# Block 0 of a fused attention and gated feed-forward kernel: another way of masking, another order of weight loads, and its projection moved

## The chip, the cores and the metric

The kernel runs on one core of one Trainium2 chip. The metric is device time in microseconds (us), from the first to the last work of the core as the device reports it; lower is better. Before the change it is 230.33 us, the median of 8 runs that lie between 230.22 and 230.37.

A core has a matrix engine (PE), a vector engine (DVE), a scalar engine (ACT), a general engine that here mostly issues transfers (POOL) and a synchronisation engine that also issues transfers (SP). Each takes its instructions in the order in which the program gives them to it.

## The reference: what is computed

Two stages. The first is causal linear attention with a decay per head, over 4 batches, 8 heads, 768 positions and 64 features per head. In blocks:

```python
intra = (q_b @ k_b.T) * Dmask          # Dmask[i,j] = lam**(i-j) where i >= j, else 0
out_b = intra @ v_b + (q_b * lam**(i+1)) @ state
state = lam**block * state + (k_b * lam**(block-1-j)).T @ v_b
```

The result, as x with 3072 rows of 512, goes through a gated feed-forward layer:

```python
out = (sigmoid(x @ w_gate) * (x @ w_val)) @ w_out     # 512 -> 1536 -> 512
```

## The kernel before, in words

The sequence is cut into 6 blocks (n = 0 to 5) of 128 positions. A block holds all 4 batches, so its feed-forward part has 512 rows. All matrix work is in bf16 with fp32 sums; the inputs are fp32 in memory and are mostly cast by the transfer that loads them.

**Attention of a block**, per batch: q and k are transposed (`t_`, line 202; from block 2 on by transposing transfers, `xbar`, line 229), copied to SBUF (`e_q`, `e_k`), multiplied to scores (`piece_s`, line 238), masked by DVE (`piece_m`, line 249, two operations of 128x512 per batch), and multiplied with v (`piece_a`, line 266). `piece_i` (line 255) adds the part that comes from the state, `piece_x` copies the sum to the feed-forward's input XT, and `piece_c` makes the state's update from `KD`, which is k times a decay, made on ACT by `piece_kd` (line 116). The decay is split over two factors: q is multiplied by lam^(i+1) (`lamq`) in `e_q`, and the mask holds lam^-(j+1) under the diagonal. From block 1 on, batches 2 and 3 have their even and odd heads swapped between the partition halves, and use `lamqs` and `decs`, copies of `lamq` and `dec` with the halves exchanged by four small transfers.

**Feed-forward of a block**: 12 groups `piece_gv` (line 308), each of 4 gate and 4 value matmuls of 128x128 by 512, a sigmoid on ACT and a product on DVE that gives HT; then 4 output tiles `piece_po` (line 324), each of 12 matmuls over all 12 HT, a copy on ACT and a transfer out. In `piece_po` the twelfth matmul of a tile needs the last HT.

**Order.** The order on every engine is written out by hand: first block 0's attention, interleaved with matmuls on zeros (`zeros`) that keep PE busy, then a list `plan` of units. A unit is a `gv` group or an output tile, with smaller pieces behind it. An instruction that waits holds back everything behind it on its engine. Block 0's groups carry block 1's attention (`behind`, lines 451 to 459); groups 0 to 3 of block 1 come next, then block 0's four output tiles, then groups 4 to 11 of block 1 (lines 478 to 490). From block 2 on the order is: 12 groups, the next block's attention, 4 output tiles.

**Loads.** POOL issues q, k, v and all weights in a written order (lines 143 to 163 and 385 to 395), and the transfers land in that order. Before a POOL transfer is issued, the eighth one before it must have landed. After block 1's v come the output weights WO in two row halves of 0.75 MB (as bf16), then k and q of block 2. `next_loads(2)` (line 403) puts block 2's two transposing transfers on SP and, after a gate on POOL, the loads of v of block 2 and of k, q of block 3. SP also issues every output transfer.

Of the kernel before, what the change touches and what calls it, by code (L numbers as in the profile page):

```python
# [16 lines left out]
def kernel(  # L17
# [23 lines left out]

    const = ctx.enter_context(tc.tile_pool(name="const", bufs=1))
    qkv = ctx.enter_context(tc.tile_pool(name="qkv", bufs=5))
    hwp = ctx.enter_context(tc.tile_pool(name="hwp", bufs=4))
    qtp = ctx.enter_context(tc.tile_pool(name="qtp", bufs=3))
    kdp = ctx.enter_context(tc.tile_pool(name="kdp", bufs=2))
    trsb = ctx.enter_context(tc.tile_pool(name="trsb", bufs=3))
# [23 lines left out]
    def swapped(n, b):  # L71
        return n > 0 and b >= NB2
# [7 lines left out]
    def rows_of(u):  # L80
        return slice(u * 64, (u + 1) * 64)
# [22 lines left out]
        nc.gpsimd.dma_start(out=WG[:, :, fs], in_=wg_r[:, :, fs])  # L104
        nc.gpsimd.dma_start(out=WV[:, :, fs], in_=wv_r[:, :, fs])

    def load_wo(f0, f1):
        fs = slice(f0, f1)
        nc.gpsimd.dma_start(out=WO[:, fs, :], in_=wo_r[:, fs, :])

    KD = {}

# [13 lines left out]
    jn = const.tile([128, 2], FP32, tag="jn")  # L126
    ip1 = const.tile([128, C], FP32, tag="ip1")
    tri = const.tile([128, C], FP32, tag="tri")
    Sb = stp.tile([128, HP, B, 64], BF16, tag="Sb", name="Sb")
    lam_bc = const.tile([128, H], FP32, tag="lam_bc")  # L130

# [2 lines left out]
    def load_hw(c, b, eng):  # L134
# [9 lines left out]
    nc.scalar.preload_act_table_set("natural_log_exp_and_others")  # L144
    nc.vector.memset(ident, 0.0)
    nc.vector.memset(Sb, 0.0)  # L146
    nc.vector.memset(tri, 0.0)
    make_identity(nc, ident, nomemset=True)
    nc.gpsimd.iota(ip1, pattern=[[1, C]], base=1, channel_multiplier=0,
                   allow_small_or_imprecise_dtypes=True)  # L150
    load(0, "k", 2, 4)
# [10 lines left out]
    load_gv(2, 4)  # L162
    load_gv(4, 6)

    lnp = const.tile([128, HP], FP32, tag="lnp")
    for u in range(2):
        us = slice(u * 64, (u + 1) * 64)
        nc.scalar.activation(lnp[us, :], lam_bc[us, u::2], AF.Ln)
    lamq = const.tile([128, HP, C], BF16, tag="lamq")
    for hp in range(HP):  # L170
        nc.scalar.activation(lamq[:, hp, :], ip1, AF.Exp, scale=lnp[:, hp:hp + 1])
    lamqs = const.tile([128, HP, C], BF16, tag="lamqs")
    lnl = const.tile([128, H], FP32, tag="lnl")
    nc.scalar.activation(lnl, lam_bc, AF.Ln)
    pk = const.tile([128, H], FP32, tag="pk")
    nc.scalar.activation(pk, lnl, AF.Exp, scale=jn[:, 0:1])
    kds = const.tile([128, H], FP32, tag="kds")
    dec = const.tile([128, HP], FP32, tag="dec")
    decs = const.tile([128, HP], FP32, tag="decs")
    mask = const.tile([128, 2, HP, C], FP32, tag="mask")  # L180

    def tables_late():
        nc.scalar.activation(kds, lnl, AF.Exp, scale=jn[:, 1:2])
        nc.scalar.activation(dec, lnp, AF.Exp, scale=float(C))
        nc.scalar.preload_act_table_set("sigmoid_and_others")
        for o, i in ((lamqs, lamq), (decs, dec)):
            for u in range(2):
                nc.sync.dma_start(out=o[rows_of(u)], in_=i[rows_of(1 - u)])

    def make_mask():  # L190
        nc.vector.tensor_tensor(
            out=mask, in0=tri.unsqueeze(1).unsqueeze(1).to_broadcast([128, 2, HP, C]),
            in1=pk.rearrange("p (hp u) -> p u hp", u=2).unsqueeze(3).to_broadcast([128, 2, HP, C]),
            op=ALU.mult)

# [4 lines left out]
    def t_(c, n, bs):  # L202
        ps = ps_at.tile([128, len(bs), HP, C], BF16, name="t" + c, tag="ps")
        for i, b in enumerate(bs):
            for hp in range(HP):
                nc.tensor.transpose(ps[:, i, hp, :], T_[c, n][:, b, 2 * hp:2 * hp + 2, :], ident)  # L206
        (tqs if c == "q" else tks)[n, bs[0]] = ps

    def e_q(n, bs):
        w = len(bs)  # L210
        src = tqs[n, bs[0]] if n < FIRST_XBAR else QT[n][:, bs[0]:bs[0] + w]
        t = trsb.tile([128, 2, HP, C], BF16, tag="QS", name="QS")
        nc.vector.tensor_tensor(out=t[:, :w], in0=src,  # L213
                                in1=(lamqs if swapped(n, bs[0]) else lamq).unsqueeze(1).to_broadcast([128, w, HP, C]), op=ALU.mult)
        for i in range(w):
            QS[n, bs[i]] = t[:, i]

# [8 lines left out]
    def cast_hw(c, b):  # L226
        nc.vector.tensor_copy(T_[c, 0][:, b], H32[c, b])
# [21 lines left out]
    def piece_m(n, b):  # L249
        MT[n, b] = mtp.tile([128, 2, HP, C], BF16, tag="MT", name="MT")  # L250
        for u in range(2):
            nc.vector.tensor_tensor(out=MT[n, b][:, u], in0=SP[n, b][u],  # L252
                                    in1=mask[:, 1 - u if swapped(n, b) else u], op=ALU.mult)

    def piece_i(n):
        for b in range(B):
# [64 lines left out]
        HT[n, ft] = htp.tile([128, TCH], BF16, tag="ht", name="ht", bufs=2 * NFT)  # L321
        nc.vector.tensor_mul(HT[n, ft], sg, vp)  # L322

    def piece_po(n, tt, cuts=(0, 512)):
        ob = osb.tile([128, DM], FP32, tag="ob", name="ob")
        rows = out[tt * S + n * C:tt * S + (n + 1) * C, :]
        for j, (c0, c1) in enumerate(zip(cuts, cuts[1:])):
            po = ps_ff.tile([128, DM], FP32, name="po", tag="ff")
            for ft in range(NFT):
                nc.tensor.matmul(po[:, :c1 - c0], lhsT=HT[n, ft][:, tt * 128:(tt + 1) * 128],  # L330
                                 rhs=WO[:, ft, c0:c1], start=(ft == 0), stop=(ft == NFT - 1))
            if j:
                nc.vector.tensor_copy(ob[:, c0:c1], po[:, :c1 - c0])
            else:
                nc.scalar.copy(ob[:, c0:c1], po[:, :c1 - c0])  # L335
            nc.sync.dma_start(out=rows[:, c0:c1], in_=ob[:, c0:c1])

# [4 lines left out]
            nc.tensor.matmul(zps, lhsT=Sb[:, 0, 0:2, :], rhs=Sb[:, 0:2], start=True, stop=True)  # L344

    zeros(9)
    for b in range(2):
        cast_hw("k", b)
        t_("k", 0, [b])
        e_k(0, [b])  # L350
        zeros(3 if b == 0 else 0)
    make_mask()
    for b in range(2):
        t_("q", 0, [b])
        e_q(0, [b])
    zeros(1)
    for b in range(2):
        piece_s(0, [b])
        piece_m(0, b)
    t_("k", 0, [2, 3])  # L360
    e_k(0, [2, 3], parts=2)
    zeros(2)
    t_("q", 0, [2, 3])
    e_q(0, [2, 3])
    tables_late()
    zeros(3)
    for b in range(2, 4):
        piece_s(0, [b])
        piece_m(0, b)
    for b in range(2):  # L370
        piece_a(0, [b])
        piece_x(0, [b], nc.scalar)
# [3 lines left out]
    zeros(1)  # L376
    piece_a(0, [3])
    piece_x(0, [3], nc.vector)
    zeros(2)

    for n in range(2):
        make_kd(n)
    load_gv(6, 8)
    load(1, "k", 0, 2)
    load(1, "q", 0, 2)
    load_gv(8, 10)
    load(1, "k", 2, 4)
    load(1, "q", 2, 4)  # L390
    load_gv(10, 12)
    load(1, "v")
    load_wo(0, 6)
    load_wo(6, 12)
    load(2, "kq")

    gates = const.tile([128, 2], BF16, tag="gates")
# [19 lines left out]
    def gv(n, ft, *more):  # L417
        unit(lambda: piece_gv(n, ft), *more)

    def po(n, tt, *more, cuts=(0, 512)):  # L420
        unit(lambda: piece_po(n, tt, cuts), *more)

    def pair(f, n, bp):
        return lambda: f(n, [2 * bp, 2 * bp + 1])
# [26 lines left out]
    behind = {ft: [] for ft in range(NFT)}  # L451
    for ft in range(4):
        behind[ft] = [kd(0, 2 * ft)]
    behind[5] = [pair(piece_c, 0, 0), pair(piece_c, 0, 1)]
    behind[7] = [trans(1, 0)]
    behind[8] = [pair(piece_s, 1, 0), m_(1, 0), m_(1, 1)]
    behind[9] = [trans(1, 1), kd(1, 0)]
    behind[10] = [pair(piece_s, 1, 1), m_(1, 2), m_(1, 3), kd(1, 2), kd(1, 4)]
    behind[11] = [kd(1, 6), att(1)]
    for ft in range(NFT):  # L460
        gv(0, ft, *behind[ft])

    for n in range(1, NSTEP):
        nx = n + 1
        more = {i: [] for i in range(NFT)}
        if nx < NSTEP:
            more[3] = [lambda nx=nx: e_q(nx, [0, 1])]
            more[4] = [pair(piece_s, nx, 0), m_(nx, 0)]
            more[5] = [m_(nx, 1), lambda nx=nx: e_q(nx, [2, 3])]
            more[7] = [pair(piece_s, nx, 1), m_(nx, 2)]  # L470
            more[8] = [m_(nx, 3)]
            more[11] = [att(nx)]
        if nx < NSTEP - 1:
            for i in range(4):
                more[6 + i].append(kd(nx, 2 * i))
        if nx < NSTEP - 1:
            more[5].append(lambda nx=nx: make_kd(nx))
        if n == 1:
            for ft in range(4):
                gv(1, ft, *[lambda: next_loads(2)] if ft == 3 else [])  # L480
            for tt in range(B):
                po(0, tt, *[lambda: next_loads(3)] if tt == 3 else [])
            gv(1, 4, *more[3])
            gv(1, 5)
            gv(1, 6, *more[4])
            gv(1, 7, *more[5])
            gv(1, 8, *more[6])
            gv(1, 9, *more[7])
            gv(1, 10, *more[8])
            gv(1, 11, *more[9], *more[10], *more[11])  # L490
        else:
            for ft in range(NFT):
                gv(n, ft, *more[ft])
        for tt in range(B):
            last = n == NSTEP - 1 and tt == B - 1
            more = [lambda n=n: next_loads(n + 3)] if tt == B - 1 and n + 3 < NSTEP else []
            po(n, tt, *more, cuts=(0, 256, 512) if last else (0, 512))

    for f, more in plan:
        f()  # L500
# [32 lines left out]
```

## Time and profile before

| what | value |
|---|---|
| median of 8 runs | 230.33 us |
| the profiled execution's own time | 230.37 us |
| its span (first to last instruction) | 228.6 us |
| PE busy | 217.5 us, 95% of the span |
| DVE, ACT, POOL busy | 100.9, 98.2, 58.4 us |
| first gate matmul | 17.99 us after the span's start |
| end of the last matmul, start of the last copy | 225.5 us |
| read from and written to device memory | 28.32 and 6.29 MB |

The profile is of one execution. A busy share is an average over stages with different limits, so the stages are read apart: up to 18 us PE often waits; from there on it is nearly always at work. The 1.77 us by which the execution's time exceeds its span are the same kind of overhead in every run of this kernel, and a change of the span is read as a change of the time.

### The profile page before, as it was taken

The page shows a single profiled execution, that of the slowest core. Times are in us where ns is not written, and L with a number is a line of the kernel's source. Part 1 is how long each engine was busy: PE and PEld are TensorE (multiplying, and loading weights), DVE is VectorE, ACT ScalarE, POOL GpSimd, SP SyncE. Part 2 cuts the span into 40 slices and gives each one's busy share as a digit, 9 for nine tenths or more (in the row PEclk, how much of TensorE's full clock was granted, in tenths as well). Part 3 has the DMA queues.
Part 4 walks back from the last instruction along what each step waited for, and adds up shares of the span by engine and source line. Part 5 has one row for each costly group of instructions (what it writes and reads, how often), then busy time and mean ns, then how long its engine had stood idle before and what let it go on. Part 6 is the DMA issues. An engine that isn't in the chain of part 4 may idle for free.

```text
span 228.6 us, 4108 instructions
## 1 busy us (share of the span) xinstructions
PE 217.5 (95%) x1642; PEld 106.9 (47%) x1668; DVE 100.9 (44%) x177; ACT 98.2 (43%) x207; POOL 58.4 (26%) x73
## 2 busy tenths in 40 slices
PE   6779999999999999999999999999999999999994
PEld 2443455544444554444554444454444454444443
DVE  2863367862038730368530368630268600243300
ACT  5465635932245832338542438642433342434221
POOL 7949669200093029103900030000000000000000
PEclk9999999999999999999999999999999999999999
DMA  7999999999999989995997739003100002100022
GB/s 114 154 163 196 175 173 176 200 181 138 217 169 154 184 124 126 207 165 103 113 152 154 165 66 93 3 22 119 46 0 3 0 33 107 46 0 0 3 92 93
DMA packets 104083, 25.31 MB, mean 111 GB/s; under 512 B 94080, under 2 KB 101120, under 8 KB 104064
## 3 DMA queue, kind: packets, MB, share of 16 engines
q0 software_dynamic: 81280, 13.90, 82.7%
q1 hardware_dynamic: 22640, 11.15, 20.8%
q8 instruction: 13, 0.21, 0.4%
q14 instruction: 6, 0.05, 0.1%
q10 hardware_dynamic: 144, 0.00, 0.0%
HBM read 28.32 MB, written 6.29 MB: 151 GB/s over the span
## 4 chain that ended last, share of the span: by engine, by line
PE 89%; DMA 3%; DVE 3%; issue 2%; POOL 1%; POOLq 0%; DVEq 0%
PE po L330 27%; PE vp L319 27%; PE gp L313 27%; DMA qb<-in_q_dram 3%; PE sp L244 3%; PE op L273 2%; DVE MT L252 2%; PE op L262 1%; PE cp L291 1%; DVE XT L283 1%; PE tq L206 1%; POOL kb L92 0%; PE tk L206 0%; DVE QS L213 0%; POOL qb L92 0%
## 5 line engine op out<-in xcount | busy, mean ns | idle before, releaser
L322 DVE TENSOR_TENSOR ht<-sg,vp 128x512 bf16<-128x512 bf16 x72 | 49.4, 686 | 105.0 <-PE vp L319 101.4
L319 PE MATMUL vp<-XT,WV 128*128 128x512 bf16 x284 | 73.5, 379 | 0.4
L313 PE MATMUL gp<-XT,WG 128*128 128x512 bf16 x274 | 72.1, 379 | 1.4 <-DVE XT L283 0.5
L316 ACT ACTIVATE sg<-gp 128x512 bf16<-128x512 f32 x72 | 43.0, 597 | 66.0 <-PE gp L313 63.3
L330 PE MATMUL po<-WO,ht 128*128 128x512 bf16 (+1 forms) x294 | 62.7, 370 | 0.4 <-issue 0.2
L330 PEld LDWEIGHTS <-ht 128*128 128x128 bf16 x300 | 29.1, 98 | 32.3
L319 PEld LDWEIGHTS <-WV 128*128 128x128 bf16 x288 | 28.2, 98 | 34.0
L313 PEld LDWEIGHTS <-WG 128*128 128x128 bf16 x288 | 27.0, 98 | 32.6 <-issue 0.8
L335 ACT COPY ob<-po 128x512 f32<-128x512 f32 (+1 forms) x24 | 13.8, 576 | 47.3 <-PE po L330 47.3
L252 DVE TENSOR_TENSOR MT<-sp,mask 128x512 bf16<-128x512 f32 x48 | 30.4, 682 | 0.6 <-PE sp L244 0.5
L121 ACT ACTIVATE kd<-kb,kds 128x128 bf16<-128x128 bf16 (+1 forms) x72 | 23.7, 403 | 0.0
L401 POOL COPY gates<-kt 128x1 bf16<-128x1 bf16 x4 | 1.3, 315 | 57.7 <-DMA kt<-kb 57.7
L283 ACT CAST XT<-op 128x512 bf16<-128x512 f32 x21 | 11.0, 596 | 5.6 <-PE op L273 5.6
L92 POOL DMA_DIRECT2D vb<-in_v_dram x7 | 10.7, 1530 | 2.6 <-issue 1.2
L98 POOL DMA_DIRECT2D qb<-in_q_dram x10 | 9.0, 913 | 3.1 <-DMA vb<-in_v_dram 2.2
L98 POOL DMA_DIRECT2D kb<-in_k_dram x10 | 8.9, 900 | 1.1 <-DMA WG<-in_moe_w_gate_dram 0.6
L344 PE MATMUL zps<-Sb 128*128 128x512 bf16 x22 | 7.4, 460 | 1.6 <-DVE Sb L146 1.5
L92 POOL DMA_DIRECT2D qb<-in_q_dram x7 | 8.4, 1200 | 0.8 <-POOLq L517 0.8
L273 PE MATMUL op<-MT,vb 128*64 128x128 bf16 x192 | 7.1, 221 | 0.4 <-DVE MT L252 0.4
L92 POOL DMA_DIRECT2D kb<-in_k_dram x6 | 7.0, 1165 | 0.0
L300 DVE SCALAR_TENSOR_TENSOR Sb<-Sb,dec,cp 128x128 bf16<-128x128 bf16 x16 | 5.5, 342 | 3.2 <-PE cp L291 3.2
L273 PEld LDWEIGHTS <-vb 128*64 128x64 bf16 x192 | 5.7, 109 | 1.5 <-DMA vb<-in_v_dram 0.4
(47 smaller groups left out, 82.6 us busy)
## 6 DMA issues: line engine op xcount, KB each, us to landing
out_dram<-ob SPq DMA_DIRECT2D x23, 256.0 KB, 2.1
vb<-in_v_dram POOLq DMA_DIRECT2D x5, 512.0 KB, 8.2
qb<-in_q_dram POOLq DMA_DIRECT2D x7, 256.0 KB, 9.4
kb<-in_k_dram POOLq DMA_DIRECT2D x6, 256.0 KB, 9.4
WO<-in_moe_w_out_dram POOLq DMA_DIRECT2D x2, 768.0 KB, 14.0
WG<-in_moe_w_gate_dram POOLq DMA_DIRECT2D x5, 256.0 KB, 8.6
WV<-in_moe_w_val_dram POOLq DMA_DIRECT2D x5, 256.0 KB, 8.8
kb<-in_k_dram POOLq DMA_DIRECT2D x10, 128.0 KB, 10.2
```

What stands on the lines that cost most here:

```text
L92: nc.gpsimd.dma_start(out=T_[c, n][:, b0:nat], in_=src[b0:nat, :, sl, :].rearrange("b h s d -> s (b h) d"))
L98: nc.gpsimd.dma_start(out=T_[c, n][:, m:b1, u::2, :], in_=src[m:b1, 1 - u::2, sl, :].rearrange("b h s d -> s (b h) d"))
L121: nc.scalar.mul(KD[n][:, at, i, :], T_["k", n][:, at, i, :], kds[:, h:h + 1])
L252: nc.vector.tensor_tensor(out=MT[n, b][:, u], in0=SP[n, b][u], in1=mask[:, 1 - u if swapped(n, b) else u], op=ALU.mult)
L273: nc.tensor.matmul(OP[n, b][rows_of(w), hp, :], lhsT=T_["v", n][:, b, h, :], rhs=MT[n, b][:, slot(n, b, h) % 2, hp, :], start=(n == 0 and ...
L283: (e.tensor_copy if e is nc.vector else e.copy)(XT[n][:, :, b, :], OP[n, b])
L313: nc.tensor.matmul(gp, lhsT=WG[:, mt, fs], rhs=x[:, mt, :], start=(mt == 0), stop=(mt == NMT - 1))
L316: nc.scalar.activation(sg, gp, AF.Sigmoid)
L319: nc.tensor.matmul(vp, lhsT=WV[:, mt, fs], rhs=x[:, mt, :], start=(mt == 0), stop=(mt == NMT - 1))
L322: nc.vector.tensor_mul(HT[n, ft], sg, vp)
L330: nc.tensor.matmul(po[:, :c1 - c0], lhsT=HT[n, ft][:, tt * 128:(tt + 1) * 128], rhs=WO[:, ft, c0:c1], start=(ft == 0), stop=(ft == NFT - 1))
L335: nc.scalar.copy(ob[:, c0:c1], po[:, :c1 - c0])
```

## The change

Five edits.

1. **Block 0's mask** (`mask0`) holds the whole decay lam^(i-j): POOL makes the distances `dij` and a table `neg` that is -30000 above the diagonal, DVE makes dij*ln(lam)+neg per head (`exponents`, 4 operations for each of two halves), ACT takes the exponential (`powers`). Block 0's q is then only copied, one batch at a time, two of the batches by ACT and two by DVE. The old mask is still made, in two halves, for the later blocks, behind groups 1 and 3 of block 0.
2. The transfers that exchange the halves of `lamq` and `dec` go from SP to ACT's queue (`swap_halves`), behind group 0 of block 0.
3. **WO is loaded by column halves**, each with all 12 row groups and 256 of the 512 columns. The first comes ahead of k and q of batches 2 and 3 of block 1, the second behind them, and v of block 1 behind both. Groups 8 to 11 of the gate and value weights move up.
4. **Block 0's projection** comes right behind its 12 groups, as 8 half tiles of 256 columns: the first halves of the 4 tiles, then the second halves. Block 1's attention is spread over groups 8 to 11 of block 0 and these half tiles, with its last part (`att(1)`) behind the last of them.
5. Block 1 then follows the order of the later blocks; its `next_loads(2)` and `next_loads(3)` come behind its groups 2 and 8. A few matmuls on zeros are left out or moved. The pool of fp32 staging tiles for k goes from 4 to 2 buffers.

The core of the diff:

```diff
-    def load_wo(f0, f1):
-        fs = slice(f0, f1)
-        nc.gpsimd.dma_start(out=WO[:, fs, :], in_=wo_r[:, fs, :])
+    def load_wo(c0, c1):
+        nc.gpsimd.dma_start(out=WO[:, :, c0:c1], in_=wo_r[:, :, c0:c1])
...
+    nc.gpsimd.iota(dij, pattern=[[1, C]], base=0, channel_multiplier=-1,
+                   allow_small_or_imprecise_dtypes=True)
+    nc.gpsimd.affine_select(out=neg, in_=neg, compare_op=ALU.is_ge, fill=-30000.0, base=0,
+                            pattern=[[1, C]], channel_multiplier=-1)
...
+    def exponents(u):
+        for hp in range(HP):
+            h = 2 * hp + u
+            nc.vector.scalar_tensor_tensor(out=mask0[:, u, hp], in0=dij, scalar=lnl[:, h:h + 1],
+                                           in1=neg, op0=ALU.mult, op1=ALU.add)
+
+    def powers(u):
+        nc.scalar.activation(mask0[:, u], mask0[:, u], AF.Exp)
...
+    def swap_halves():
+        for u in range(2):
+            o, i = rows_of(u), rows_of(1 - u)
+            nc.scalar.dma_start(out=lamq2[o, 1], in_=lamq2[i, 0])
+            nc.scalar.dma_start(out=dec2[o, 1], in_=dec2[i, 0])
...
+        if n == 0:
+            (nc.scalar.copy if eng is nc.scalar else nc.vector.tensor_copy)(t[:, :w], src)
...
     load_gv(6, 8)
+    load_gv(8, 10)
     load(1, "k", 0, 2)
     load(1, "q", 0, 2)
-    load_gv(8, 10)
+    load_gv(10, 12)
+    load_wo(0, 256)
     load(1, "k", 2, 4)
     load(1, "q", 2, 4)
-    load_gv(10, 12)
+    load_wo(256, 512)
     load(1, "v")
-    load_wo(0, 6)
-    load_wo(6, 12)
     load(2, "kq")
...
+    behind[0].append(swap_halves)
+    behind[1].append(lambda: make_mask(0))
+    behind[3].append(lambda: make_mask(1))
     behind[5] = [pair(piece_c, 0, 0), pair(piece_c, 0, 1)]
-    behind[7] = [trans(1, 0)]
-    behind[8] = [pair(piece_s, 1, 0), m_(1, 0), m_(1, 1)]
-    behind[9] = [trans(1, 1), kd(1, 0)]
-    behind[10] = [pair(piece_s, 1, 1), m_(1, 2), m_(1, 3), kd(1, 2), kd(1, 4)]
-    behind[11] = [kd(1, 6), att(1)]
+    behind[8] = [trans(1, 0)]
+    behind[9] = [pair(piece_s, 1, 0), m_(1, 0)]
+    behind[10] = [m_(1, 1), kd(1, 0)]
+    behind[11] = [kd(1, 2)]
     for ft in range(NFT):
         gv(0, ft, *behind[ft])
+    after = {(0, 2): [trans(1, 1)], (0, 3): [pair(piece_s, 1, 1), m_(1, 2)],
+             (1, 0): [m_(1, 3), kd(1, 4)], (1, 1): [kd(1, 6)], (1, 3): [att(1)]}
+    for j in range(2):
+        for tt in range(B):
+            po(0, tt, *after.get((j, tt), []), c=(256 * j, 256 * (j + 1)))
```

The start of block 0, after the edit, reads:

```python
zeros(9); exponents(0); powers(0)
cast_hw("k", 0); t_("k", 0, [0]); e_k(0, [0])
exponents(1); cast_hw("k", 1); zeros(3); powers(1)
t_("q", 0, [0]); e_q(0, [0], nc.scalar); t_("q", 0, [1]); e_q(0, [1], nc.vector)
t_("k", 0, [1]); e_k(0, [1])
piece_s(0, [0]); piece_m(0, 0); piece_s(0, [1]); piece_m(0, 1)
t_("k", 0, [2, 3]); e_k(0, [2, 3], parts=2); tables_late(); zeros(2)
t_("q", 0, [2]); e_q(0, [2], nc.vector); t_("q", 0, [3]); e_q(0, [3], nc.scalar)
nc.scalar.preload_act_table_set("sigmoid_and_others"); zeros(1)
for b in range(2, 4): piece_s(0, [b]); piece_m(0, b)
zeros(2)
```

and goes on as before, without the last `zeros(2)`.

More of the change, by code (lines that the diff above doesn't have):

```diff
@@ L43 @@
     qkv = ctx.enter_context(tc.tile_pool(name="qkv", bufs=5))
-    hwp = ctx.enter_context(tc.tile_pool(name="hwp", bufs=4))
+    hwp = ctx.enter_context(tc.tile_pool(name="hwp", bufs=2))
     qtp = ctx.enter_context(tc.tile_pool(name="qtp", bufs=3))
@@ L128 @@
     tri = const.tile([128, C], FP32, tag="tri")
+    dij = const.tile([128, C], FP32, tag="dij")
+    neg = const.tile([128, C], FP32, tag="neg")
     Sb = stp.tile([128, HP, B, 64], BF16, tag="Sb", name="Sb")
@@ L146 @@
     nc.vector.memset(Sb, 0.0)
+    nc.vector.memset(neg, 0.0)
     nc.vector.memset(tri, 0.0)
     make_identity(nc, ident, nomemset=True)
+    nc.gpsimd.iota(dij, pattern=[[1, C]], base=0, channel_multiplier=-1,
+                   allow_small_or_imprecise_dtypes=True)
+    nc.gpsimd.affine_select(out=neg, in_=neg, compare_op=ALU.is_ge, fill=-30000.0, base=0,
+                            pattern=[[1, C]], channel_multiplier=-1)
     nc.gpsimd.iota(ip1, pattern=[[1, C]], base=1, channel_multiplier=0,
@@ L163 @@
     load_gv(4, 6)
+    lnl = const.tile([128, H], FP32, tag="lnl")
+    nc.scalar.activation(lnl, lam_bc, AF.Ln)
     lnp = const.tile([128, HP], FP32, tag="lnp")
@@ L168 @@
         nc.scalar.activation(lnp[us, :], lam_bc[us, u::2], AF.Ln)
-    lamq = const.tile([128, HP, C], BF16, tag="lamq")
+    lamq2 = const.tile([128, 2, HP, C], BF16, tag="lamq2")
+    lamq, lamqs = lamq2[:, 0], lamq2[:, 1]
     for hp in range(HP):
         nc.scalar.activation(lamq[:, hp, :], ip1, AF.Exp, scale=lnp[:, hp:hp + 1])
-    lamqs = const.tile([128, HP, C], BF16, tag="lamqs")
-    lnl = const.tile([128, H], FP32, tag="lnl")
-    nc.scalar.activation(lnl, lam_bc, AF.Ln)
     pk = const.tile([128, H], FP32, tag="pk")
-    nc.scalar.activation(pk, lnl, AF.Exp, scale=jn[:, 0:1])
@@ L177 @@
     kds = const.tile([128, H], FP32, tag="kds")
-    dec = const.tile([128, HP], FP32, tag="dec")
-    decs = const.tile([128, HP], FP32, tag="decs")
+    dec2 = const.tile([128, 2, HP], FP32, tag="dec2")
+    dec, decs = dec2[:, 0], dec2[:, 1]
+    mask0 = const.tile([128, 2, HP, C], FP32, tag="mask0")
     mask = const.tile([128, 2, HP, C], FP32, tag="mask")
+    def exponents(u):
[3 more added lines that the diff above has]
+                                           in1=neg, op0=ALU.mult, op1=ALU.add)
@@ L182, in tables_late @@
+    def powers(u):
+        nc.scalar.activation(mask0[:, u], mask0[:, u], AF.Exp)
     def tables_late():
+        nc.scalar.activation(pk, lnl, AF.Exp, scale=jn[:, 0:1])
         nc.scalar.activation(kds, lnl, AF.Exp, scale=jn[:, 1:2])
         nc.scalar.activation(dec, lnp, AF.Exp, scale=float(C))
[L185 to L188, printed above, removed]
@@ L190, in make_mask @@
-    def make_mask():
+    def swap_halves():
[3 more added lines that the diff above has]
+            nc.scalar.dma_start(out=dec2[o, 1], in_=dec2[i, 0])
+    def make_mask(u):
         nc.vector.tensor_tensor(
-            out=mask, in0=tri.unsqueeze(1).unsqueeze(1).to_broadcast([128, 2, HP, C]),
-            in1=pk.rearrange("p (hp u) -> p u hp", u=2).unsqueeze(3).to_broadcast([128, 2, HP, C]),
-            op=ALU.mult)
+            out=mask[:, u], in0=tri.unsqueeze(1).to_broadcast([128, HP, C]),
+            in1=pk[:, u::2].unsqueeze(2).to_broadcast([128, HP, C]), op=ALU.mult)
@@ L207, in t_, with e_q @@
         (tqs if c == "q" else tks)[n, bs[0]] = ps
-    def e_q(n, bs):
+    def e_q(n, bs, eng=None):
         w = len(bs)
@@ L212, in e_q @@
         t = trsb.tile([128, 2, HP, C], BF16, tag="QS", name="QS")
-        nc.vector.tensor_tensor(out=t[:, :w], in0=src,
-                                in1=(lamqs if swapped(n, bs[0]) else lamq).unsqueeze(1).to_broadcast([128, w, HP, C]), op=ALU.mult)
+        if n == 0:
+            (nc.scalar.copy if eng is nc.scalar else nc.vector.tensor_copy)(t[:, :w], src)
+        else:
+            nc.vector.tensor_tensor(
+                out=t[:, :w], in0=src,
+                in1=(lamqs if swapped(n, bs[0]) else lamq).unsqueeze(1).to_broadcast([128, w, HP, C]),
+                op=ALU.mult)
         for i in range(w):
@@ L252, in piece_m @@
             nc.vector.tensor_tensor(out=MT[n, b][:, u], in0=SP[n, b][u],
-                                    in1=mask[:, 1 - u if swapped(n, b) else u], op=ALU.mult)
+                                    in1=(mask if n else mask0)[:, 1 - u if swapped(n, b) else u],
+                                    op=ALU.mult)
     def piece_i(n):
@@ L322, in piece_gv, with piece_po @@
         nc.vector.tensor_mul(HT[n, ft], sg, vp)
[L324 to L336, printed above, removed]
+    OB = {}
+    def piece_po(n, tt, c0, c1, eng):
+        if (n, tt) not in OB:
+            OB[n, tt] = osb.tile([128, DM], FP32, tag="ob", name="ob")
+        po = ps_ff.tile([128, DM], FP32, name="po", tag="ff")
+        for ft in range(NFT):
+            nc.tensor.matmul(po[:, :c1 - c0], lhsT=HT[n, ft][:, tt * 128:(tt + 1) * 128],
+                             rhs=WO[:, ft, c0:c1], start=(ft == 0), stop=(ft == NFT - 1))
+        o = OB[n, tt][:, c0:c1]
+        (eng.copy if eng is nc.scalar else eng.tensor_copy)(o, po[:, :c1 - c0])
+        nc.sync.dma_start(out=out[tt * S + n * C:tt * S + (n + 1) * C, c0:c1], in_=o)
     zps = ps_ff.tile([128, DM], FP32, name="zps", tag="ff")
@@ L346 @@
     zeros(9)
[L347 to L359, printed above, removed]
+    exponents(0)
+    powers(0)
+    cast_hw("k", 0)
+    t_("k", 0, [0])
+    e_k(0, [0])
+    exponents(1)
+    cast_hw("k", 1)
+    zeros(3)
+    powers(1)
+    t_("q", 0, [0])
+    e_q(0, [0], nc.scalar)
+    t_("q", 0, [1])
+    e_q(0, [1], nc.vector)
+    t_("k", 0, [1])
+    e_k(0, [1])
+    piece_s(0, [0])
+    piece_m(0, 0)
+    piece_s(0, [1])
+    piece_m(0, 1)
     t_("k", 0, [2, 3])
     e_k(0, [2, 3], parts=2)
+    tables_late()
     zeros(2)
[L363 to L366, printed above, removed]
+    t_("q", 0, [2])
+    e_q(0, [2], nc.vector)
+    t_("q", 0, [3])
+    e_q(0, [3], nc.scalar)
+    nc.scalar.preload_act_table_set("sigmoid_and_others")
+    zeros(1)
     for b in range(2, 4):
@@ L369 @@
         piece_m(0, b)
+    zeros(2)
     for b in range(2):
@@ L378 @@
     piece_x(0, [3], nc.vector)
-    zeros(2)
     for n in range(2):
@@ L418, in gv, with po @@
         unit(lambda: piece_gv(n, ft), *more)
-    def po(n, tt, *more, cuts=(0, 512)):
-        unit(lambda: piece_po(n, tt, cuts), *more)
+    def po(n, tt, *more, c=(0, DM), eng=nc.scalar):
+        unit(lambda: piece_po(n, tt, *c, eng), *more)
     def pair(f, n, bp):
@@ L475 @@
                 more[6 + i].append(kd(nx, 2 * i))
-        if nx < NSTEP - 1:
             more[5].append(lambda nx=nx: make_kd(nx))
         if n == 1:
[L479 to L493, printed above, removed]
-        for tt in range(B):
-            last = n == NSTEP - 1 and tt == B - 1
-            more = [lambda n=n: next_loads(n + 3)] if tt == B - 1 and n + 3 < NSTEP else []
-            po(n, tt, *more, cuts=(0, 256, 512) if last else (0, 512))
+            more[2].append(lambda: next_loads(2))
+            more[8].append(lambda: next_loads(3))
+        for ft in range(NFT):
+            gv(n, ft, *more[ft])
+        for tt in range(B):
+            if n == NSTEP - 1 and tt == B - 1:
+                po(n, tt, c=(0, 256))
+                po(n, tt, c=(256, 512), eng=nc.vector)
+            else:
+                more = [lambda n=n: next_loads(n + 3)] if tt == B - 1 and n + 3 < NSTEP else []
+                po(n, tt, *more)
     for f, more in plan:
```

## The prediction, made blind

> **What bounds the kernel now.** I read the page's busy slices first, then the chain that ended last in its early windows, then the instructions in order of time by engine, and the transfers' times to landing. In the slices a digit is a tenth, for 5.7 us each:
>
> ```profile
> PE   6779999999999999999999999999999999999994
> DMA  7999999999999989995997739003100002100022
> ```
>
> PE is full from slice 4 on, so past 18 us only PE work and PE gaps count. But the transfers are saturated up to about 57 us (slice 10): what PE needs in that time must have landed. The chain's pieces (start, length):
>
> ```profile
> 4.64 7.67 DMA qb<-in_q_dram
> ...
> 14.20 2.48 DVE MT L252 x4
> 16.68 0.01 issue
> 16.70 0.43 PE op L273 x8
> 17.13 0.02 issue
> 17.15 0.70 DVE XT L283
> 17.86 0.14 issue
> 17.99 1.02 PE gp L313 x4
> ```
>
> The start hangs on q of batches 2 and 3, then on four masks in a row. Later PE has one gap worth naming, at block 1's attention (PE in order of time):
>
> ```profile
> 42.64 0.40 PE L262 MATMUL op<-QS,Sb 64*64 64x128 bf16 x3
> 43.42 0.60 PE L262 MATMUL op<-QS,Sb 64*64 64x128 bf16 x29 [0.39 <-DVE MT L252]
> 43.95 1.08 PE L273 MATMUL op<-MT,vb 128*64 128x128 bf16 x32
> 44.87 0.92 PE L291 MATMUL cp<-vb,kd 128*64 128x64 bf16 x32
> 45.98 1.04 PE L313 MATMUL gp<-XT,WG 128*128 128x512 bf16 x3 [0.19 <-DVE XT L283]
> ```
>
> L262 needs 1.32 us here (42.63 to 43.95) because the masks of batches 2 and 3 are late; in the next block it takes 0.57 (78.48 to 79.05). POOL shows when loads land, since an issue waits for the eighth one before it:
>
> ```profile
> 27.05 0.87 POOL L98 DMA_DIRECT2D qb<-in_q_dram  x1 [0.47 <-DMA WV<-in_moe_w_val_dram]
> 29.00 0.75 POOL L104 DMA_DIRECT2D WG<-in_moe_w_gate_dram  x1 [1.07 <-DMA kb<-in_k_dram]
> 30.44 0.74 POOL L105 DMA_DIRECT2D WV<-in_moe_w_val_dram  x1 [0.69 <-DMA qb<-in_q_dram]
> 42.56 0.88 POOL L98 DMA_DIRECT2D qb<-in_q_dram  x1 [2.24 <-DMA vb<-in_v_dram]
> ```
>
> So WV of groups 6 and 7 landed at 26.8 (its own row: issued 17.73, 9.0 to landing), k and q of block 1's batches 0, 1 at 28.7 and 30.2, v of block 1 at 42.3. And ACT and SP:
>
> ```profile
> 39.09 1.28 ACT L121 ACTIVATE kd<-kb,kds 128x128 bf16<-128x128 bf16 x4
> 40.27 0.58 ACT L316 ACTIVATE sg<-gp 128x512 bf16<-128x512 f32 x1
> ```
>
> ```profile
> 54.28 3.26 SPq L232 DMA_TRANSPOSE kt<-kb  x1
> 57.73 2.97 SPq L232 DMA_TRANSPOSE qt<-qb  x1
> ```
>
> ACT runs `kd` of block 1 ahead of a sigmoid, without a wait; k had landed by 35. The two transposes start when k and q of block 2 have landed (54.2, 57.1) and land 6.3 and 4.9 us after their issue.
>
> [...] The trace's loads land in issue order; outputs beside loads are not seen before 57 us. [...]
>
> **The change, part by part.** Call 0.25 MiB of fp32 in memory a unit. From the landings above: k, q: (30.2-26.8)/4 = 0.85 us a unit; gate and value weights 8 to 11, whose first four units land at 32.8 (issued 21.69, 11.1 to landing): 2.6/4 = 0.66; WO: landings 46.1 and 50.4 behind v's 42.3, 8.1/12 = 0.67. A WO column half has rows of 1 KB, as the gate weights of two groups have, so 0.66.
>
> *Start (edits 1, 2).* POOL issues k of batches 2, 3 some 0.55 us later (the iota on L149 takes 0.25, the select on L155 0.30). The transfers are saturated from 4.5 us and k's descriptors wait some 4 us in line, so I take 0 (0 to +0.5). The exchange of `lamq`, 128 KB between 5.7 and 13.5, leaves the early traffic: v lands up to 0.3 earlier. [...] q's copies: per batch 0.4 on DVE (half of 0.69) instead of 0.69 for two, so masks 2 and 3 start at 12.36+0.35+0.4+0.45, about 13.6 for 14.2, but v of batches 2, 3 lands at 16.0 and `piece_a` waits for it: first gate matmul at 17.8 (-0.2; -0.4 to +0.4). The omitted zeros ran while PE waited: 0. ACT's four transfer issues at 0.42 to 0.6 (its `lam_bc`, SP's `lamqs`) are 2 us behind group 0; the sequencer does them while sigmoid and `kd` (1.5 us) run: 0.5 late against a slack of 0.9 on the third PSUM tile: 0, at worst +0.9. Half masks behind groups 1 and 3: DVE has 1.0 us free per group, 0.
>
> *Middle (edits 3, 4).* Up to group 11, PE has from before's starts 12 groups of 1.73, `piece_c` 0.63, one `trans` 0.89, one `piece_s` 0.55: group 11 ends at 40.9. The first WO half lands at 26.8 + 4x0.66 + 4x0.85 + 4x0.66 + 6x0.66 = 39.4: in time. k of batches 2, 3 of block 1 now lands *behind* it: +2x0.85 = **41.1**. `kd(1,0)` stands behind group 10 on ACT, reaches its second operation at 39.5, and holds back the sigmoid of group 11. From landing L: three more `kd` operations to L+1.0, sigmoid L+1.65, product L+2.4, twelfth matmul of the first half tile L+2.5 = 43.6. Without the wait PE would be there at 40.9-0.1+11x0.11, about 42.1. So PE stops about 1.4 us, and whatever the start gained or lost is swallowed.
>
> From there: 7 half tiles at 1.31 (the last tile shows 222.91, 224.22, 225.53, against 2.59 for a whole; 8 cost 0.12 extra), `trans` 0.89, `piece_s` 0.55, `att(1)` 0.05+0.57+2.03 = 2.65 (from 43.95 to 45.98 in before; the mask wait, 0.8, is gone), 5 groups of block 1, 8.65. Group 4 of block 1 is done at L+2.6+21.9 = 65.6. Before had done the same work at 65.0. The second WO half lands at 41.1+1.7+4.0 plus three outputs, 47.8, needed at 49; v of block 1 at some 51.7, needed at 55: in time.
>
> *Transposes (edit 5).* The 8 outputs of 128 KB now run beside the loads. Rows of outputs alone move 394 GB/s (62 to 63 us), so 0.33 us each, 2.6 in all: k and q of block 2 land at 56.8 and 59.8, transposes are issued at 56.9 and 60.2, q's lands at 64.5 to 65.1; with the copy 0.69, block 2's first scores can start at 65.3 to 66.0, where PE wants them at 65.6. That adds 0 to 0.4; I take 0.15. Later loads stand behind this, some 2 us late with over 5 us to spare.
>
> Sum: 65.6+0.15-65.0 = **+0.75 us**. Afterwards the work is the same. Span 228.6+0.75 = 229.35; with 1.77 around it 231.12, against the profiled 230.37; against the median 230.33, 231.1.
>
> **The rivals.** *k lands early enough* (ends faster): if L is below 39.7 the wait for `kd` vanishes, and if the transposed q lands below 63.5 too, what is left is -0.2 (start) -0.8 (masks) +0.12 (half tiles) = -0.9: 229.5. It decides at L = 40.0; for it, column halves could move faster than gate weights. Against it, loads land in order and k has 18 units ahead of it after 26.8. *The transposes become the bound*: if outputs and loads disturb each other more than by their bytes, or a transpose issue takes longer, q's lands at 66.5 or later, scores start at 67.3: +2.0, 232.3. For it: all 8 outputs fall into the saturated time. *Gain and wait cancel*: L at 40 to 40.9: within 0.46 us of before.
>
> **How the numbers follow.** Forecast 0.62 (its own range 230.8 to 231.7), early k 0.13 (229.2 to 229.8), transposes 0.10 (231.8 to 232.6), cancelling 0.15 (229.9 to 230.8). L is known to about 0.6 us and passes one to one into the time. 0.2% is 0.46 us, about what a measurement of this kernel can tell from no change: faster 0.13, same 0.15, slower 0.72. The range 230.0 to 232.2 leaves out the early case and half of the transposes' one.
>
> **What would show it.** Right: ACT idle before a `kd` instruction at 39.5 until k's landing near 41.1; PE idle about 1.4 us at the end of the first half tile, released by the product of group 11; no mask wait in `att(1)`; first gate matmul at 17.4 to 18.4; transposes issued 2 to 3 us later than before. Wrong: k landing before 40, PE waiting for the second WO half, group 1's sigmoid over 1 us late behind ACT's transfer issues, or PE waiting over 1 us for block 2's scores.

## The result

The changed kernel takes 231.43 us, the median of 11 runs (231.13 to 232.80), against 230.29 (230.22 to 230.39, 31 runs). The ratio of the means is 1.0064, with a 95% interval of 1.0053 to 1.0075: slower. The 11 times fall into two groups, 7 from 231.13 to 231.48 and 4 from 232.35 to 232.80. The profiled execution, with 232.88 us and a span of 231.1, is of the upper kind: its times after 44 us are later than those of most executions.

The slices of the page, as before 40 to the span:

```profile
PE   6779999599999999999999999999999999999994
PEclk9999999889999999999999999999999999999999
DMA  7999999999969949993992659002100003100022
```

In the kernel before, the clock's row is:

```profile
PEclk9999999999999999999999999999999999999999
```

PE has a new hole in slice 8 (40 to 46 us), and the clock granted to it is down in slices 8 and 9, which it never was before. First the start, PE and its weight loads in order of time:

```profile
14.60 0.25 PEld L296 LDWEIGHTS <-vb 128*64 128x64 bf16 x8 [0.42 <-DMA vb<-in_v_dram]
...
16.57 1.02 PE L336 MATMUL gp<-XT,WG 128*128 128x512 bf16 x4 [0.88 <-DVE XT L306]
```

The first gate matmul comes 1.42 us earlier than before (17.99), behind v's landing. Then the hole, all engines in order of time, the rows that make it up:

```profile
39.61 1.36 PE L354 MATMUL po<-WO,ht 128*128 128x256 bf16 x11
...
41.15 0.98 ACT L120 ACTIVATE kd<-kb,kds 128x128 bf16<-128x128 bf16 x3 [3.05 <-DMA kb<-in_k_dram]
...
42.04 0.57 ACT L339 ACTIVATE sg<-gp 128x512 bf16<-128x512 f32 x1
...
42.65 0.69 DVE L345 TENSOR_TENSOR ht<-sg,vp 128x512 bf16<-128x512 bf16 x1 [2.61 <-ACT sg L339]
...
43.39 4.57 PE L354 MATMUL po<-WO,ht 128*128 128x256 bf16 x25 [2.42 <-DVE ht L345]
```

PE does 11 of the 12 terms of the first half tile and stops for 2.42 us. The rows above it are the reason, read upwards: the product waits for the sigmoid, the sigmoid stands behind `kd` on ACT, and `kd` waits 3.05 us for k, which landed at 41.13 by the trace. The last row also shows what came after: 25 matmuls in 4.57 us, 183 ns each, where a half tile's matmul took 109 in the kernel before (12 in 1.31 us). The windows of one us say why (the third number from the end is the granted clock; the two behind it, the transfers' share and GB/s, are not used here):

```profile
43.00:44.00 1.00, 0.61 (x6) 0.56 (x7) 0.33 (x1) 1.00 (x4) 1.00 (x2) 1.00 1.47 195
44.00:45.00 1.00, 1.00 (x9) 0.77 (x7) 0.00 (x0) 0.08 (x1) 0.54 (x1) 0.66 1.53 194
45.00:46.00 1.00, 1.00 (x7) 0.67 (x6) 0.00 (x0) 0.37 (x1) 0.00 (x0) 0.50 2.16 166
46.00:47.00 1.00, 1.00 (x7) 0.67 (x6) 0.00 (x0) 0.00 (x0) 0.00 (x0) 0.50 2.44 159
47.00:48.00 1.00, 1.00 (x9) 0.79 (x8) 0.00 (x0) 0.00 (x1) 0.00 (x0) 0.63 2.47 158
```

The clock is still full when PE starts again; from 44.3 to 47.7 us, 3.4 us by the trace, it is half. SP's transposes, and PE's first scores of block 2, in order of time:

```profile
57.01 3.21 SPq L254 DMA_TRANSPOSE kt<-kb  x1
60.39 1.87 SPq L254 DMA_TRANSPOSE qt<-qb  x1
...
67.33 0.62 PE L266 MATMUL sp<-QS,kt 64*128 64x128 bf16 x16
```

The transposes are 2.7 us later than before (54.28, 57.73). Before had done the same PE work as this at 65.0.

### The profile page after: what moved, and what is told of

Same layout as the page of the kernel before. It is cut to its first block, busy times and chain, and to the rows that moved or that the text cites. A ratio compares the mean times of both kernels' runs of the same rounds, so it can differ in the third digit from the quotient of the medians.

```text
span 231.1 us, 4227 instructions
## 1 busy us (share of the span) xinstructions
PE 219.0 (95%) x1689; PEld 112.0 (48%) x1713; DVE 101.9 (44%) x186; ACT 100.6 (44%) x215; POOL 59.6 (26%) x75
## 4 chain that ended last, share of the span: by engine, by line
PE 79%; DMA 13%; POOL 3%; issue 2%; DVE 1%; ACT 1%; POOLq 0%
PE po L354 27%; PE vp L342 23%; PE gp L336 22%; DMA kb<-in_k_dram 6%; DMA WG<-in_moe_w_gate_dram 5%; DMA vb<-in_v_dram 3%; PE sp L266 2%; PE op L296 2%; PE op L285 1%; PE cp L314 1%; POOL WV L105 1%; POOL qb L92 1%; POOL vb L92 1%; DVE XT L306 1%; POOL kb L92 0%
## 5 line engine op out<-in xcount | busy, mean ns | idle before, releaser
L354 PE MATMUL po<-WO,ht 128*128 128x512 bf16 (+1 forms) x343 | 65.2, 349 | 2.7 <-DVE ht L345 2.4
L354 PEld LDWEIGHTS <-ht 128*128 128x128 bf16 x348 | 34.2, 100 | 31.5 <-DVE ht L345 2.7
L357 ACT COPY ob<-po 128x512 f32<-128x512 f32 (+1 forms) x28 | 14.4, 515 | 45.0 <-PE po L354 45.0
L432 POOL COPY gates<-kt 128x1 bf16<-128x1 bf16 x4 | 0.7, 186 | 57.8 <-DMA kt<-kb 57.8
L323 DVE SCALAR_TENSOR_TENSOR Sb<-Sb,dec,cp 128x128 bf16<-128x128 bf16 x32 | 8.6, 342 | 3.3 <-PE cp L314 3.3
```

Source lines behind the costliest of these rows:

```text
L357: (eng.copy if eng is nc.scalar else eng.tensor_copy)(o, po[:, :c1 - c0])
```

## The experiments

**1. Take `kd` out of the sigmoid's way.**

```diff
-    behind[10] = [m_(1, 1), kd(1, 0)]
-    behind[11] = [kd(1, 2)]
+    behind[10] = [m_(1, 1)]
-    after = {(0, 2): [trans(1, 1)], (0, 3): [pair(piece_s, 1, 1), m_(1, 2)],
+    after = {(0, 0): [kd(1, 0)], (0, 1): [kd(1, 2)], (0, 2): [trans(1, 1)], (0, 3): [pair(piece_s, 1, 1), m_(1, 2)],
```

> The changed kernel with kd(1,0) and kd(1,2) moved from behind groups 10 and 11 to behind the first two half tiles, so that no sigmoid stands behind the wait for k. Theory (ACT's queue held back by k's late landing is what costs the time): ACT's 3.0 us wait before kd and PE's 2.4 us stop at the first half tile are gone, PE runs the first halves from 39.6 on, then waits some 1 us for the second WO half (landing near 47.3), and block 2's first scores come near 64.6 instead of 67.3: 229.9 us (229.4 to 230.4). Rival (the loads as a whole set the pace, the stop only moves to the second WO half or to the transposes): 231.0 or more.

Measured: 231.30 us (6 runs, 230.72 to 232.68), ratio 1.005 (1.003 to 1.007). The time is the rival's (five of the six executions lie above 231.0), and so is its reason. What the theory says of ACT is right as far as it goes: the sigmoid no longer stands behind `kd`, and PE runs the first half tiles from 39.36 without a stop. But see where PE stops now (ACT's sigmoid of group 11, then PE in order of time):

```profile
38.70 0.60 ACT L339 ACTIVATE sg<-gp 128x512 bf16<-128x512 f32 x1 [1.13 <-PE gp L336]
```

```profile
39.36 4.09 PE L354 MATMUL po<-WO,ht 128*128 128x256 bf16 x36
...
46.81 5.40 PE L354 MATMUL po<-WO,ht 128*128 128x256 bf16 x48 [0.59 <-DMA WO<-in_moe_w_out_dram]
...
65.49 0.62 PE L266 MATMUL sp<-QS,kt 64*128 64x128 bf16 x16 [1.95 <-DVE QS L233]
```

Where the changed kernel stops 2.42 us for ACT, this one stops 0.59 for the second WO half and 1.95 for block 2's transposed q. The transposed q landed at 64.63, in the changed kernel at 64.68: its landing did not move with what PE does.

**2. Load k ahead of the first WO half.**

```diff
-    load_wo(0, 256)
     load(1, "k", 2, 4)
+    load_wo(0, 256)
```

> The changed kernel with k of block 1's batches 2 and 3 loaded ahead of the first WO half. Theory: k lands near 38, ACT does not wait, the first WO half lands near 41.1 and PE waits for it 1.6 us instead of 2.4, with the sigmoid and product of group 11 long done: 230.0 us (229.6 to 230.6). Rival (what counts is when all of WO half, k and q have landed, in whatever order): 231.2, as the changed kernel.

Measured: 231.17 us (231.13 to 231.59), ratio 1.0044 (1.0031 to 1.0057). ACT no longer waits, and PE waits for WO and then for the same q (PE in order of time):

```profile
40.58 4.10 PE L354 MATMUL po<-WO,ht 128*128 128x256 bf16 x36 [0.76 <-DMA WO<-in_moe_w_out_dram]
...
65.62 0.62 PE L266 MATMUL sp<-QS,kt 64*128 64x128 bf16 x16 [1.50 <-DVE QS L233]
```

The number is the rival's, its reason is not: the second stop, not the sum of WO, k and q, sets the time, as run 8 confirms. In both runs a second bound lay close behind the first. The forecast had named it, 0 to 0.4 us of it, and had the transposed q at 64.5 to 65.1; my expectation for run 1 had the first scores at 64.6, 0.9 us too early. K's transpose took 4.06 and 4.75 us on SP when issued at 56.09 and 55.38, beside the loads, and q's transpose waits for q anyway, which the trace has landing at 60.25 and 60.40 (57.12 before).

**3. Keep PE busy in the stop.** Twenty more matmuls, whose sum is thrown away:

```diff
         po = ps_ff.tile([128, DM], FP32, name="po", tag="ff")
+        for ft in (range(NFT - 2) for _ in range(2 if (n, tt, c0) == (0, 0, 0) else 0)):
+            for f in ft:
+                nc.tensor.matmul(po[:, :c1 - c0], lhsT=HT[n, f][:, tt * 128:(tt + 1) * 128],
+                                 rhs=WO[:, f, c0:c1], start=(f == 0), stop=(f == NFT - 3))
         for ft in range(NFT):
```

> The changed kernel with 20 further matmuls (two passes over the first ten terms of the first half tile, thrown away by the real pass) that fill 2.2 us of PE's stop; nothing else is changed. Theory (the stop of 2.4 us lets the clock of PE be halved for some 3.4 us in part of the executions, which makes the upper group of times at 232.4 to 232.9): granted clock 1.00 in every run and all times between 231.0 and 231.5. Rival (the upper group comes from the transfers or from something else): times up to 232.8 remain.

Measured: 231.18 us (5 runs, 231.05 to 231.40), ratio 1.0041 (1.0029 to 1.0053); no run above 231.40, granted clock 0.998 to 1.00. The window that had clock 0.50 in the changed kernel, and the stop that is left:

```profile
45.00:46.00 1.00, 1.00 (x15) 0.92 (x13) 0.00 (x0) 0.09 (x1) 0.00 (x0) 1.00 2.16 166
```

```profile
65.86 0.62 PE L266 MATMUL sp<-QS,kt 64*128 64x128 bf16 x16 [0.54 <-DVE QS L233]
```

More work, and no time of the upper group. Five runs without it are not many: with 5 of 12 executions of the changed kernel in the upper group, the profiled one included, five in a row without one would come by chance about 7 times in 100. The other kernels point the same way: the 29 executions of runs 2, 3, 4 and 8, in whose traces PE stops for 1.50 us at most after the start, all have a clock of 0.997 or more. ACT still waits for k (2.67 us), and the time is that of the changed kernel at full clock. In the changed kernel's runs the clock and the time go together too: 0.993 in the four upper ones and the profiled one, 0.997 to 1.00 in the seven lower ones. This run is also the best look at a changed kernel at full clock: scores of block 2 at 65.86, held up 0.54 us by q. K landed at 40.70 here and the transposed q at 64.99.

**4. The old start, with the new middle** (edits 1 and 2 undone).

> The changed kernel with the old start (edits 1 and 2 undone), the new load order and the new place of the projection kept. Theory (the wait for k swallows what the start gains): PE starts 1.4 us later, k lands 0.4 to 0.7 later, PE's stop is shorter than in the changed kernel, and the time is only 0 to 0.7 us above it: 231.3 to 232.1. Rival (the start's gain is kept to the end): 1.4 us above the changed kernel, 232.7 or more.

Measured: 231.98 us (231.76 to 232.11), ratio 1.0074 (1.0062 to 1.0086): 0.55 us above the changed kernel's median, with a start 1.28 later (PE in order of time):

```profile
17.85 1.02 PE L312 MATMUL gp<-XT,WG 128*128 128x512 bf16 x4 [0.34 <-DVE XT L282]
...
43.68 2.90 PE L330 MATMUL po<-WO,ht 128*128 128x256 bf16 x25 [1.47 <-DVE ht L321]
```

PE's stop is 1.47 instead of 2.42 us and ends 0.3 later. The wait for k swallows a good part of the start, but not all of it, because k itself lands later with the old start: at 41.42, where the changed kernel has 41.13 and run 3 40.70. Against run 3, which is at full clock, the time is 0.8 us longer.

**5. The new start, with the old middle** (edits 1 and 2 alone).

> The kernel before with the new start alone (edits 1 and 2), its own load order and its own place of the projection kept. Theory (the start is worth 1.4 us, and the moved projection with its load order throws it away and costs 0.9 more): first gate matmul near 16.6, about 0.5 us lost on q of batches 2 and 3 and on the weights of group 10, which now come just in time, block 1's first gate matmul near 45.0: 229.4 us (229.0 to 229.8). Rival (before's loads are as much in the way, so the start's gain is swallowed here too): 230.0 or more.

Measured: 229.16 us (228.95 to 229.42), ratio 0.9954 (0.9942 to 0.9967), faster than the kernel before and the changed one. PE in order of time:

```profile
16.57 1.02 PE L337 MATMUL gp<-XT,WG 128*128 128x512 bf16 x4 [0.88 <-DVE XT L307]
...
38.45 1.04 PE L343 MATMUL vp<-XT,WV 128*128 128x512 bf16 x4 [0.36 <-DMA WV<-in_moe_w_val_dram]
...
44.69 1.04 PE L337 MATMUL gp<-XT,WG 128*128 128x512 bf16 x4 [0.27 <-DVE XT L307]
```

Of 1.42 us at the start, 1.29 are left at block 1's first group (45.98 before). So edits 3 to 5 cost 2.27 us on top of this start (231.43 less 229.16), and 2.0 at full clock (run 3's 231.18 less 229.16).

**6. The exchange of the halves moved alone** (edit 2). Here it goes from `tables_late`, on SP's queue, to a function of its own behind group 0, on ACT's:

```diff
-        for o, i in ((lamqs, lamq), (decs, dec)):
-            for u in range(2):
-                nc.sync.dma_start(out=o[rows_of(u)], in_=i[rows_of(1 - u)])
+    def swap_halves():
+        for u in range(2):
+            for o, i in ((lamqs, lamq), (decs, dec)):
+                nc.scalar.dma_start(out=o[rows_of(u)], in_=i[rows_of(1 - u)])
...
+    behind[0].append(swap_halves)
```

> The kernel before with the exchange of the halves of lamq and dec moved alone, from SP early on to ACT's queue behind group 0 (edit 2); mask, q's scaling and everything else as before. Theory A (the start comes early because these 128 KB no longer run between the first loads): q of batches 2 and 3 lands near 11.0 instead of 12.3, v near 14.4 instead of 16.0, first gate matmul near 16.8, time 229.3 to 229.7. Theory B (it comes from the masks, which start earlier with q copied per batch): loads land at most 0.4 us earlier, first gate matmul 17.6 to 18.0, time 230.0 to 230.3.

Measured: 230.09 us (21 runs, 229.90 to 230.21), ratio 0.9990 (0.9983 to 0.9996). The time is theory B's, but the loads are neither's: q of batches 2, 3 landed at 11.75 and v at 15.29, between the two; PE in order of time:

```profile
17.42 1.02 PE L315 MATMUL gp<-XT,WG 128*128 128x512 bf16 x4 [0.34 <-DVE XT L285]
```

So the exchange is worth 0.57 us at the start (0.7 us on v's landing) and 0.20 in the medians of the time; the other 0.85 us of the start come only together with edit 1, where v lands at 14.34 to 14.35 (the changed kernel and run 5). Why edit 1 speeds up the loads is open. What differs: q of batches 0, 1 lands at 7.4 with the new start and at 8.1 with the old, POOL issues k of batches 2, 3 at 3.51 instead of 3.07, and DVE's casts of k take 0.41 us instead of 0.98 and 0.87. The staging pool of 2 instead of 4 buffers went with edit 1 in every run. No run measured the pool alone, or edit 1 without edit 2.

**7. A try at more.** As 5, with block 1's loads in the order of need and its transposes and scores moved behind groups 8 to 10.

```diff
     load_gv(6, 8)
+    load_gv(8, 10)
     load(1, "k", 0, 2)
     load(1, "q", 0, 2)
-    load_gv(8, 10)
     load(1, "k", 2, 4)
     load(1, "q", 2, 4)
-    load_gv(10, 12)
+    load_gv(10, 11)
+    load_gv(11, 12)
...
-    behind[7] = [trans(1, 0)]
-    behind[8] = [pair(piece_s, 1, 0), m_(1, 0), m_(1, 1)]
-    behind[9] = [trans(1, 1), kd(1, 0)]
-    behind[10] = [pair(piece_s, 1, 1), m_(1, 2), m_(1, 3), kd(1, 2), kd(1, 4)]
-    behind[11] = [kd(1, 6), att(1)]
+    behind[8] = [trans(1, 0)]
+    behind[9] = [kd(1, 0), pair(piece_s, 1, 0), m_(1, 0), trans(1, 1), m_(1, 1)]
+    behind[10] = [pair(piece_s, 1, 1), m_(1, 2), m_(1, 3), kd(1, 2)]
+    behind[11] = [kd(1, 4), kd(1, 6), att(1)]
```

> A try at better than both: the new start, the projection where it was before, and block 1's loads in the order of need: gate and value weights 8 and 9, k and q of batches 0, 1, then of 2, 3, weights 10, weights 11, v; block 1's transposes behind groups 8 and 9, its scores behind 9 and 10. Theory (loads bound block 0 only through the order in which PE wants them): no PE stop over 0.5 us from 16.6 to 41, block 1's first gate matmul near 44.3: 228.6 us (228.2 to 229.2). Rival (the loads' sum, not their order, is the bound): 229.4, as with the new start alone.

Measured: 229.33 us (229.29 to 229.44), ratio 0.996 (0.9948 to 0.9973), no better than 5. The number is the rival's, its reason is not: no wait of PE for a load is left after the start, and block 1's first group starts at 44.90 all the same, behind copies of `op`:

```profile
44.42 0.44 PE L315 MATMUL cp<-vb,kd 128*64 128x64 bf16 x16 [0.49 <-ACT XT L307]
```

From 39.5 to 44.5 DVE works without a pause (products, four masks of 0.62 us, two copies), and ACT's copy stands behind eight `kd`. By the trace the bound there is their work, which the expectation had not added up; no run took work away from them to test it.

**8. The first wait shortened, the second removed.** As 2, with block 2's copies of q and scores two groups later (`d = 2 if n == 1 else 0` added to their five places in `more`).

> The changed kernel with k of block 1's batches 2 and 3 loaded ahead of the first WO half, and block 2's copies of q and its scores two groups later, where they stood before. Theory (with k's wait gone the transposes of block 2, late by the outputs ahead of them and beside the loads, are the last bound, 1.5 us): PE has no stop at these scores: 229.7 us (229.4 to 230.2). Rival (another wait takes its place): 230.8 or more.

Measured: 229.75 us (14 runs, 229.52 to 230.04), ratio 0.9978 (0.9970 to 0.9986), 1.42 below run 2, as expected. Of the first wait 0.77 us are left, for WO as in run 2; the scores have none (PE in order of time):

```profile
40.62 4.10 PE L354 MATMUL po<-WO,ht 128*128 128x256 bf16 x36 [0.77 <-DMA WO<-in_moe_w_out_dram]
...
67.55 0.62 PE L266 MATMUL sp<-QS,kt 64*128 64x128 bf16 x16
```

So the changed kernel is slower by two waits, one behind the other. With the first cut down and the second gone it takes 0.54 us less than the kernel before; with the same start, the old middle (run 5) still takes 0.59 less than that.

## Why the prediction was right, and where not

The forecast of 231.1 stands against 231.43 for all runs and 231.13 to 231.48 for those at full clock. The path that it foresaw is the one that the trace shows. That the number came so close is in part luck: terms that were 0.4 to 1.2 us off either cancelled or stood ahead of a wait. Step by step:

- **ACT's queue behind k: right.** The stop was to end at 43.6 and ended at 43.39. That the sigmoid does not pass the waiting `kd`, on which the forecast rested, the traces show: the gate matmuls of group 11 end at 38.9, `kd` waits 3.05 us for k until 41.15, and the sigmoid comes at 42.04, right behind it; in run 1, where no `kd` stands ahead of it, it comes at 38.70.
- **k's landing: right to 0.4 us, and closer than that by luck.** L was to be 41.1; the profiled execution has 41.13, and 39.43 for the WO half ahead of it, foreseen 39.4. Up to 78 us the loads whose landing the two traces have land in the order of issue, and each of POOL's 11 waits for a load in the changed kernel, 0.32 to 2.15 us, ends with the landing of the eighth load before it. But the sum starts from landings of the kernel before, with its old start, and the new start brings the loads forward: in runs 1 and 3, which load in the same order, k landed at 40.66 and 40.70. In the profiled execution one load on the way, the value weights of groups 10 and 11, landed at 36.13 instead of 34.88 and made up for it.
- **The start: right in sign, mis-sized.** -0.2 for -1.42. The first gate matmul comes some 2.1 us behind v's landing in the forecast, 2.2 in the trace; the term that failed is v's landing, put up to 0.3 earlier and measured 1.64 earlier (14.34 for 15.98). I counted the exchange by its bytes; run 6 shows 0.7 us for it, and 0.95 more arrive with edit 1. The four `exponents` of a half take 1.17 and 1.13 us on DVE and the two `powers` 0.61 and 0.63 on ACT; the casts of k start at 5.29 and 6.68 (5.07 and 6.35 before) and are done by 7.10, ahead of q's transposes at 7.54.
- **"Whatever the start gained or lost is swallowed": right in part**, and it is why the mis-sized start did little harm. PE's stop is 2.42 instead of 1.4 us, 1.0 longer, for a start 1.2 earlier than forecast. But the forecast let k's landing stand still; it moves with the start, and run 4, with a start 1.28 later, loses 0.55 to 0.8.
- **Mask wait in `att(1)` gone: right.** From the first of its matmuls (55.99) to block 1's first group (58.59) it takes 2.60, foreseen 2.65, before 3.35 (42.63 to 45.98).
- **The transposes: right in time, too small in weight.** q's was to land at 64.5 to 65.1 and landed at 64.68, in run 3 at 64.99. But at full clock (run 3) PE wants the scores early enough to wait 0.54 us, for which I took 0.15. There k lands 0.4 earlier than forecast and this wait is 0.4 longer: the two cancel, and the scores start at 65.86, foreseen 65.75. In runs 1 and 2 this second wait takes nearly all that the first one gives back. As a cause, then, the wait for k is half the story; the other half is that q of block 2 lands 3 us later than before. The forecast put 2.6 for it, the bytes of the outputs. Against run 5, with the same start and the outputs behind the loads, it is some 4 us (56.32 there, 60.25 and 60.40 in runs 1 and 2). That the outputs beside the loads do this is argued, not shown: the order of the loads changes with them, and no run parts the two.
- **Two slips in the working**, without effect on the forecast: its own figures put PE at the twelfth matmul at 42.0 without the wait, so the stop at 1.6 and not 1.4 us; and scores at 67.3, in the rival of the transposes, would be 2.3 above 65.0, not 2.0.
- **The second WO half, ACT's transfer issues, the later loads: right to cost nothing** here. The first two of ACT's four issues (17.77 and 18.33) run beside the sigmoid of group 0 and `kd`; the other two end at 20.23, 1.2 us after `kd`, and delay group 1's sigmoid (20.27) by 0.9 us instead of 0.5, without a stop of PE.
- **Not foreseen: the clock.** It puts 4 of the 11 runs 1.2 us higher. No step of the sum looked at what a stop does to the matmuls after it. Half the clock for 3.4 us is 1.7 us of work (25 matmuls took 4.57 us there, 2.90 in run 4); that only 1.2 show fits the wait for q, 0.54 us in run 3 and absent in the profiled execution.
- **A rest of 0.2 us** lies behind the last output: it lands 0.9 us before the span's end in the kernel before, 1.1 in run 3. It stays unexplained.

## What to carry to other kernels

An instruction that waits for a load costs what stands behind it in its queue, so read what is queued there before moving a load past its user: here a decay of k, wanted much later, waited 3.05 us and stopped a sigmoid that the next matmul needed. When a wait is found and removed, ask at once which landing comes next; here it lay half a microsecond behind and took the gain, and only work on both paid. When a sum of many terms comes out right, check the terms: here two that were 0.4 us off cancelled. A gain ahead of a wait for a load is worth little more than what it moves that load's landing: the same start was worth 1.1 us in one order of work and, with the other middle, where k landed 0.29 to 0.72 earlier by it, 0.55 to 0.8.

## What the runs showed of the hardware that was not expected

- A stop of PE of 2.42 us was followed, in the profiled execution, by half the clock for 3.4 us, which began 0.9 us after PE had started again. 25 matmuls of 128x256 took 4.57 us there; at full clock (run 4, after a stop of 1.47 us) the same 25 took 2.90. By their mean clock of 0.993, 4 of the 11 other executions had the same. With the 20 thrown-away matmuls of run 3 none of five had it. One of run 1's six runs, with a stop of 1.95 us in its profile, came in at 232.68 with a granted clock of 0.990; none of the 29 executions with stops up to 1.50 us (runs 2, 3, 4, 8) did. Why some executions have it and others not was not found.
- The transposing transfer of k occupied SP for 3.2 us in the changed kernel, where it was issued late, and for 4.1 to 5.2 when issued earlier, beside more of the loads (runs 1 to 4 and 8). Issuing it up to 1.6 us earlier did not make it end earlier (60.22; 60.15 and 60.13 in runs 1 and 2). In the nine traces that have the landing of block 2's last q (before, runs 1 to 8) it left SP within 0.5 us of that landing, issued 2.8 to 5.4 us ahead of it. Why was not tested.
- Two transfers of 64 KB from SBUF to SBUF among the first loads delayed v by 0.7 us (run 6), twice what their bytes would take at the rate of the output rows (an estimate of 0.33 us for 128 KB, from the 394 GB/s of the kernel before at 62 to 63 us).
